# Reading the moving operand of every large product as pairs of columns 256 apart

## The chip, the cores and the metric

The kernel runs on one core of a Trainium2 chip. The metric is device time in microseconds (us) of one execution, the median of several. Every matmul goes to TensorE (PE in the profile), which keeps one operand in place (the weights, `lhsT`) and lets the other stream past it (the moving operand, `rhs`), one column after the other, into PSUM. VectorE (DVE), ScalarE (ACT) and GpSimd (POOL) do the rest, and SyncE (SP) issues all DMA transfers of this kernel.

## What is computed

A recurrent attention layer, followed by a two-layer network with SiLU between the layers. In the reference, cut to what matters:

```python
B, H, S, D = 4, 8, 768, 64
for t in range(S):
    state = gamma * state + einsum('bhd,bhe->bhde', k[:, :, t], v[:, :, t])
    y[:, :, t] = scale * einsum('bhd,bhde->bhe', q[:, :, t], state)
x = y.transpose(0, 2, 1, 3).reshape(B * S, H * D)      # 3072 x 512
h = x @ w_in                                           # 512 x 2048
out = (h * sigmoid(h)) @ w_out                         # 2048 x 512, out is 3072 x 512
```

## The kernel before

**Tokens.** The 768 steps are cut into 6 chunks c of 128 steps. One chunk of all 4 batch rows b makes 512 tokens, in the order b, then step: token number n of a chunk is step n mod 128 of batch row n div 128.

**Attention** (`stage_t`, `stage_s`, `stage_a`, `stage_y`, lines 471 to 606) works on units (c, b) with many small matmuls of 64 by 64 and leaves x transposed in `xt[c]`: 128 partitions, 4 slices `kk` of the 512 features, 512 tokens.

**Exact products out of a faster number type.** Every fp32 operand is split into a high part, a low part and a third part that combines them (`split_steps` for the weights, `split_x` for x, `split` for the middle values). Each product is made of three matmuls in fp32r: high and low go into one PSUM bank (`ha`, or `oa` at the end), the third into another (`hb`, `ob`), and the result is `ha * ONE_E - hb`.

**First product** (`multiply`, lines 743 to 751; `multiply_part`, lines 938 to 942, for the first few, which are woven into the attention by hand). For each chunk c and each of the 16 slices f of 128 middle features, 12 matmuls of 128x512: three parts by four `kk`. The weights are `w_sb[f]`, the moving operand is `xt[c][:, i, kk, :]`, 512 tokens. `close_steps` (lines 769 to 782) copies `ha` out on ACT, subtracts `hb` on DVE, applies SiLU on ACT, and SP writes the 128x512 result to DRAM (`gd`, line 791).

**Second product** (lines 1225 to 1249). For each chunk c and slice f, the middle values are read back (`gr`, line 804), split into three parts (`split`, lines 836 to 841), and each of the 4 blocks of 128 tokens (`ts(b, C)`) serves as weights of three matmuls of 128x512, whose moving operand is `wo[f][:, i, :]`, the 512 output columns. After 16 slices f, block b is complete in the banks `oa` and `ob`. ACT copies `oa` out (line 1288), DVE subtracts `ob` (line 1289), and SP stores 128 rows of 2 KB (line 1294). As the blocks are the batch rows, the 128 rows of a block are 128 consecutive rows of the output.

**The end** (lines 1251 to 1283). In the last chunk the last two slices f are multiplied block by block (line 1267), so that the first blocks are copied out while PE works on the others. The last block is done as a left and a right half of 256 columns, each finished by one DVE instruction (line 1281) and stored by its own DMA (line 1283).

**Order.** PE's order of instructions is written out by hand. In the first 56 us the other engines' order is, too; later their queues follow from calls like `tc.issue_after`. In the second half SP alternates between reading `gr`, which waits until a buffer has been split, and storing finished blocks.

Of the kernel before, what the change touches and what calls it, by code (L numbers as in the profile page):

```python
# [18 lines left out]
AF = mybir.ActivationFunctionType  # L19
ALU = mybir.AluOpType  # L20
# [10 lines left out]
ONE_E = 1.0 + EPS  # L31
# [3 lines left out]
def kernel(  # L35
# [28 lines left out]
    nc = tc.nc  # L64
    B, H, S, D = q.shape
    DM, DF = moe_w_in.shape
    C = 128
# [9 lines left out]
    scale = 1.0 / math.sqrt(D)  # L77
# [54 lines left out]
    def split_w(*of):  # L132
# [2 lines left out]
        yield  # L135
        list(steps)


    units = [(c, b) for c in range(NC) for b in range(B)]
    kqv = {"k": {}, "q": {}, "v": {}}  # L140
# [172 lines left out]
    def fill(out, n, start=True):  # L313

        cols = out.shape[-1] // 128
        for _ in range(n):
            nc.tensor.matmul(out, lhsT=zero, rhs=zero.unsqueeze(1).to_broadcast([128, cols, 128]),
                             start=start, stop=True, skip_group_check=True)
# [25 lines left out]
    for j in range(2):  # L344
        for a in range(HP):
            nc.scalar.activation(out=decay[:, j, a, :], in_=lag[:, :D], func=AF.Exp,
                                 scale=float(lg[2 * a + j]))
# [10 lines left out]
    for h in range(H):  # L358
        nc.scalar.activation(out=gk[:, 0, h : h + 1], in_=pos, func=AF.Exp,
                             scale=float(-lg[h]))  # L360
# [22 lines left out]
    xt, kt, qt, am = {}, {}, {}, {}  # L383
# [8 lines left out]
    def banks(tag, name, n=2):  # L392
        return ps_u.tile([128, n, 512], FP32, tag=tag, name=name)
# [3 lines left out]
    def turn(name):  # L397
        turns[0] += 1
        return ps_h.tile([128, 512], FP32, tag=f"h{turns[0] % 3}", name=name)
# [340 lines left out]
    def product_in(c, f):  # L740
        close_in(c, f, *multiply(c, f))

    def multiply(c, f):
        ha, hb = turn(f"ha_{c}_{f}"), turn(f"hb_{c}_{f}")
        fill(ha, FILL_P.get((c, f), 0))
        for i in range(3):
            for kk in range(KIN):
                nc.tensor.matmul(hb if i == 2 else ha, lhsT=w_sb[f][:, i, ts(kk, 128)],  # L748
                                 rhs=xt[c][:, i, kk, :], start=kk == 0 and i != 1,
                                 stop=kk == KIN - 1 and i != 0)  # L750
        return ha, hb

# [33 lines left out]
    def put_g(keep, of=None):  # L786
        of = pending if of is None else of
        while len(of) > keep:
            c, f, g = of.pop(0)
            with tc.issue_after(last[0]) if of is later else ExitStack():  # L790
                last[:] = stored[:] = [nc.sync.dma_start(out=g_dram[c, f], in_=g).ins]
# [3 lines left out]
    got, ready, wo, w_got = {}, {}, {}, {}  # L795
# [31 lines left out]
    def split(n):  # L827
        if n >= len(order):
            return
        c, f = order[n]  # L830
        get(n + G_AHEAD)
        g = got.pop(n)
        if f % 4 == 0:
            blocks[n // 4] = xpool.tile([128, 3, 4, NT], FP32R, tag="xt", name=f"gs_{c}_{f}")
        t = blocks[n // 4][:, :, f % 4, :]
        nc.scalar.activation(out=t[:, 0, :], in_=g, func=AF.Copy, scale=HALF)  # L836
        high = t[:, 0, :].bitcast(FP32)
        nc.vector.tensor_tensor(out=t[:, 1, :], in0=g, in1=high, op=ALU.subtract)  # L838
        nc.vector.scalar_tensor_tensor(out=t[:, 2, :], in0=t[:, 1, :].bitcast(FP32),  # L839
                                       scalar=-1.0 / EPS, in1=high,  # L840
                                       op0=ALU.mult, op1=ALU.add)
        ready[n] = t
# [95 lines left out]
    def multiply_part(c, f, into, steps):  # L938
        for i, kk in [(i, kk) for i in range(3) for kk in range(KIN)][steps]:
            nc.tensor.matmul(into[i == 2], lhsT=w_sb[f][:, i, ts(kk, 128)],  # L940
                             rhs=xt[c][:, i, kk, :], start=kk == 0 and i != 1,
                             stop=kk == KIN - 1 and i != 0)

    def PP(n, i):
# [277 lines left out]
                        split(f - NF + S_AHEAD)  # L1222
    put_g(0)

    for c in range(NC):
        acc = []
        for b in range(B):
            if b < 2:
                u = banks("sy"[b], f"o{b}_{c}")
                acc.append([u[:, i] for i in range(2)])  # L1230
            else:
                acc.append([turn(f"oa{b}_{c}"), turn(f"ob{b}_{c}") if b == 2 else
                            banks("q", f"ob{b}_{c}", 1)[:, 0]])
        early_f = NF if c < NC - 1 else NF - 2
        for f in range(NF):
            n = c * NF + f
            split(n + S_AHEAD)
            if n < 4:
                w_out(NF - 4 + n)
            t = ready[n]  # L1240
            if f >= early_f:
                continue
            for b in range(B):
                gh, glo, gm = (t[:, i, ts(b, C)] for i in range(3))
                oa, ob = acc[b]
                for o, g, i in (oa, gh, 0), (oa, glo, 1), (ob, gm, 2):
                    nc.tensor.matmul(o, lhsT=g, rhs=wo[f][:, i, :], start=f == 0 and i != 1,  # L1247
                                     stop=f == NF - 1 and i != 0 or
                                     (b, f, i) == (B - 1, early_f - 1, 1))

        ends = []
        if early_f < NF:
            left, right = (ts(i, DM // 2) for i in range(2))
            halves_of = [one.tile([128, DM // 2], FP32, tag="qt", name=f"o_{x}", bufs=3)
                         for x in ("left", "right")]
            nc.scalar.activation(out=halves_of[0], in_=acc[B - 1][0][:, left], func=AF.Copy,
                                 scale=ONE_E)
            last_left = banks("s", "oa_left")[:, 0]
            for b in (0, 1, B - 1, 2):
                ends.append((b, acc[b][1], (2,), slice(None)))  # L1260
                if b < B - 1:
                    ends.append((b, acc[b][0], (0, 1), slice(None)))
            ends += [(B - 1, last_left, (0, 1), left), (B - 1, acc[B - 1][0], (0, 1), right)]
        for b, o, parts, cols in ends:
            for f in range(early_f, NF):
                for i in parts:
                    nc.tensor.matmul(o[:, cols], lhsT=ready[c * NF + f][:, i, ts(b, C)],  # L1267
                                     rhs=wo[f][:, i, cols],
                                     start=o is last_left and (f, i) == (early_f, 0),
                                     stop=f == NF - 1 and i != 0,  # L1270
                                     skip_group_check=cols != slice(None))
        for b in range(B):
            oa, ob = acc[b]
            rows = ds(b * S + c * C, C)
            if c == NC - 1 and b == B - 1:
                nc.vector.tensor_tensor(out=halves_of[0], in0=halves_of[0], in1=ob[:, left],
                                        op=ALU.subtract)
                nc.scalar.copy(out=halves_of[1], in_=ob[:, right])
                for x, o, cols, op in ((last_left, halves_of[0], left, ALU.add),
                                       (oa, halves_of[1], right, ALU.subtract)):  # L1280
                    nc.vector.scalar_tensor_tensor(out=o, in0=x[:, cols], scalar=ONE_E, in1=o,
                                                   op0=ALU.mult, op1=op)
                    nc.sync.dma_start(out=out[rows, cols], in_=o)
                continue
            o = one.tile([128, DM], FP32, tag=("kt", "qt")[b % 2], name=f"o_{c}_{b}",
                         bufs=(2, 3)[b % 2])
            if c < NC - 1:
                nc.scalar.activation(out=o, in_=oa, func=AF.Copy, scale=ONE_E)  # L1288
                nc.vector.tensor_tensor(out=o, in0=o, in1=ob, op=ALU.subtract)
            else:  # L1290
                nc.scalar.copy(out=o, in_=ob)
                nc.vector.scalar_tensor_tensor(out=o, in0=oa, scalar=ONE_E, in1=o,
                                               op0=ALU.mult, op1=ALU.subtract)
            nc.sync.dma_start(out=out[rows, :], in_=o)


# [28 lines left out]
```

## Time and profile before

| | |
|---|---|
| time, median of 3 runs (lowest, highest) | 612.83 us (611.51, 613.1) |
| span of the profiled execution, first to last instruction | 609.7 us |
| difference of that median to the span, taken as what lies around the span | 3.1 us |
| PE busy with matmuls | 602.0 us, 99% of the span, 5509 instructions |
| DVE, ACT, POOL busy | 65%, 54%, 6% |
| DMA engines, mean share in 40 slices | 90% or more at the start, 30 to 50% in the second half |

The page of the profile does not give the profiled execution's own time; its span is the number that is compared. In lines of groups stand the kernel line, the engine, the operation, the tile written and the tiles read, the shape and the number of instructions, then the time in sum and the mean of one in nanoseconds. Matmuls are pipelined, so the duration of one (about 390 ns) is longer than the distance from one to the next; the distance has to be read from start times.

### The profile page before, as it was taken

To read this page: it belongs to the slowest core of one execution; us is meant where nothing else is said; L and a number is where in the kernel's file an instruction comes from. 1 tells how busy PE (TensorE), PEld (TensorE's weight loads), DVE (VectorE), ACT (ScalarE), POOL (GpSimd) and SP (SyncE) were. 2 spreads that over 40 slices of the span, in tenths; PEclk is the share of its full clock that TensorE was granted. 3 is DMA by queue.
4 is the path that set the end of the run, shared out by engine and by line. 5 is a ranking of instruction groups with operands and counts; after the bars stand their busy time and mean duration, and the time that the engine had idled before them with its cause. 6 is when DMAs were issued, how large, how long until landed. Compare 5 with 4: busy or idle time off the path is not lost.

```text
span 609.7 us, 13719 instructions
## 1 busy us (share of the span) xinstructions
PE 602.0 (99%) x5509; PEld 496.7 (81%) x5509; DVE 395.3 (65%) x672; ACT 326.4 (54%) x607; POOL 33.9 (6%) x89
## 2 busy tenths in 40 slices
PE   8999999999999999999999999999999999999997
PEld 6787888888888888888888888888888888888886
DVE  3888898678876766766699775635454553645632
ACT  7788777678766677666789622221221312313211
POOL 3000110100031111210000000000000000000000
PEclk9999999999999999999999999999999999999999
DMA  9997878876899699898777532524433432533301
GB/s 192 215 211 187 192 208 265 240 236 205 256 248 211 163 274 262 244 279 264 263 267 246 161 124 88 188 69 119 158 91 117 138 119 89 161 115 103 104 1 69
DMA packets 144334, 108.89 MB, mean 179 GB/s; under 512 B 101136, under 2 KB 109584, under 8 KB 144272
## 3 DMA queue, kind: packets, MB, share of 16 engines
q1 hardware_dynamic: 144272, 108.03, 62.6%
q8 instruction: 43, 0.70, 0.5%
q14 instruction: 19, 0.16, 0.1%
HBM read 66.06 MB, written 36.70 MB: 169 GB/s over the span
## 4 chain that ended last, share of the span: by engine, by line
PE 94%; SPq 2%; DMA 2%; ACT 1%; issue 0%; DVE 0%; POOL 0%; DVEq 0%; POOLq 0%
PE ha L748 28%; PE o L1247 21%; PE oa L1247 14%; PE hb L748 14%; PE ob L1247 7%; PE y L576 4%; SPq L166 2%; PE sc L518 2%; PE sc L528 2%; DMA kqv<-in_v_dram 1%; PE ha L940 1%; DMA wf<-in_moe_w_in_dram 1%; PE hb L940 0%; PE o L1267 0%; PE kp L486 0%; PE qp L486 0%
## 5 line engine op out<-in xcount | busy, mean ns | idle before, releaser
L748 PE MATMUL ha<-xt,wi 128*128 128x512 f32 x736 | 184.2, 392 | 0.0
L748 PEld LDWEIGHTS ha<-xt,wi 128*128 128x128 f32 x736 | 136.7, 188 | 29.0
L1247 PE MATMUL o<-wo,gs 128*128 128x512 f32 x564 | 143.1, 389 | 0.0
L836 ACT ACTIVATE gs<-gr 128x512 fp32r<-128x512 f32 x96 | 53.3, 621 | 139.0 <-issue 138.0
L1247 PEld LDWEIGHTS o<-wo,gs 128*128 128x128 f32 x564 | 105.8, 188 | 22.0
L838 DVE TENSOR_TENSOR gs<-gr,gs 128x512 fp32r<-128x512 f32 x96 | 62.1, 684 | 94.2 <-ACT gs L836 94.2
L1247 PE MATMUL oa<-wo,gs 128*128 128x512 f32 x376 | 115.7, 389 | 0.0
L748 PE MATMUL hb<-xt,wi 128*128 128x512 f32 x368 | 98.3, 389 | 0.0
L776 DVE TENSOR_TENSOR g<-g,hb 128x512 f32<-128x512 f32 x87 | 59.5, 684 | 52.7 <-ACT g L771 39.1
L1247 PEld LDWEIGHTS oa<-wo,gs 128*128 128x128 f32 x376 | 70.6, 188 | 14.7
L748 PEld LDWEIGHTS hb<-xt,wi 128*128 128x128 f32 x368 | 69.1, 188 | 14.4
L1247 PE MATMUL ob<-wo,gs 128*128 128x512 f32 x188 | 73.1, 389 | 0.0
L781 ACT ACTIVATE g<-g 128x512 f32<-128x512 f32 x87 | 54.9, 631 | 33.4 <-DVE g L776 33.2
L771 ACT ACTIVATE g<-ha 128x512 f32<-128x512 f32 x87 | 51.8, 596 | 26.7 <-PE ha L748 19.9
L839 DVE SCALAR_TENSOR_TENSOR gs<-gs 128x512 fp32r<-128x512 f32 x96 | 62.0, 683 | 0.1
L1247 PEld LDWEIGHTS ob<-wo,gs 128*128 128x128 f32 x188 | 35.3, 188 | 7.3
L205 ACT ACTIVATE ca<-wf 128x512 f32<-128x512 f32 x32 | 21.5, 673 | 7.3 <-DVE cs L218 2.9
L536 DVE TENSOR_TENSOR am<-sc,decay 128x512 f32<-128x512 f32 x24 | 16.5, 687 | 11.8 <-PE sc L528 10.5
L1288 ACT ACTIVATE o<-o 128x512 f32<-128x512 f32 x10 | 6.0, 600 | 33.4 <-PE o L1247 33.0
L218 DVE SCALAR_TENSOR_TENSOR cs<-ca,cs 128x512 uint32<-128x512 uint32 x32 | 23.1, 722 | 0.9
L576 PE MATMUL y<-qt,mid 64*64 64x64 f32 x376 | 19.5, 220 | 0.6 <-issue 0.5
L653 DVE SCALAR_TENSOR_TENSOR xt<-xt 128x512 fp32r<-128x512 f32 x28 | 19.7, 714 | 0.6
(137 smaller groups left out, 606.3 us busy)
## 6 DMA issues: line engine op xcount, KB each, us to landing
gr<-gd SPq DMA_DIRECT2D x96, 256.0 KB, 2.7
gd<-g SPq DMA_DIRECT2D x87, 256.0 KB, 3.6
wf<-in_moe_w_out_dram SPq DMA_DIRECT2D x16, 512.0 KB, 4.4
out_dram<-o SPq DMA_DIRECT2D x23, 256.0 KB, 2.1
wf<-in_moe_w_in_dram SPq DMA_DIRECT2D x16, 256.0 KB, 4.2
wf<-in_moe_w_in_dram SPq DMA_DIRECT2D x32, 128.0 KB, 3.9
kf<-in_k_dram SPq DMA_DIRECT2D x16, 256.0 KB, 4.1
qf<-in_q_dram SPq DMA_DIRECT2D x16, 256.0 KB, 4.1
```

Of the source, the lines that this page charges most:

```text
L205: top = nc.scalar.activation(out=a.bitcast(FP32), in_=hi.bitcast(FP32), func=AF.Abs, scale=2.0 ** -3).ins
L218: nc.vector.scalar_tensor_tensor(out=s, in0=a, scalar=3, in1=s, op0=ALU.logical_shift_left, op1=ALU.bitwise_xor)
L576: i = nc.tensor.matmul(to[ts(e, D), o, a, :], lhsT=lhsT, rhs=rhs, start=key not in started, stop=True, skip_group_check=True).ins
L653: nc.vector.scalar_tensor_tensor(out=x[2], in0=x[1].bitcast(FP32), scalar=-1.0 / EPS, in1=x[0].bitcast(FP32), op0=ALU.mult, op1=ALU.add)
L748: nc.tensor.matmul(hb if i == 2 else ha, lhsT=w_sb[f][:, i, ts(kk, 128)], rhs=xt[c][:, i, kk, :], start=kk == 0 and i != 1, stop=kk == KIN ...
L771: copied[:] = [nc.scalar.activation(out=hs, in_=ha, func=AF.Copy, scale=ONE_E).ins]
L776: taken_out[:] = [nc.vector.tensor_tensor(out=hs, in0=hs, in1=hb, op=ALU.subtract).ins]
L781: nc.scalar.activation(out=hs, in_=hs, func=AF.Silu)
L836: nc.scalar.activation(out=t[:, 0, :], in_=g, func=AF.Copy, scale=HALF)
L838: nc.vector.tensor_tensor(out=t[:, 1, :], in0=g, in1=high, op=ALU.subtract)
L839: nc.vector.scalar_tensor_tensor(out=t[:, 2, :], in0=t[:, 1, :].bitcast(FP32), scalar=-1.0 / EPS, in1=high, op0=ALU.mult, op1=ALU.add)
L1247: nc.tensor.matmul(o, lhsT=g, rhs=wo[f][:, i, :], start=f == 0 and i != 1, stop=f == NF - 1 and i != 0 or (b, f, i) == (B - 1, early_f - 1 ...
```

## The change

`woven` reads a row of 512 columns in the order 0, 256, 1, 257, 2, 258 and so on: pairs of columns that lie 256 apart, which in fp32r is 1,024 bytes. All large products take their moving operand that way. The number of matmuls, their shapes, their weights and their order on PE stay the same.

The consequences are carried along. In the first product the tokens of a chunk come out in woven order and stay so in `gd`: a block of 128 columns then holds 64 steps of two batch rows, alternating (rows b div 2 and 2 + b div 2, steps (b mod 2) * 64 onward). So a finished block of the second product is stored by two DMAs, one from the even and one from the odd partitions, 64 rows of 2 KB each (`store_out`). In the second product the output columns come out woven in PSUM; the instructions of ACT and DVE that copy them out read every second column (`unwoven`) and write two runs of 256 (`apart_cols`). The left half of the last block now holds columns 0 to 127 and 256 to 383, so its two DMAs store pieces of 512 bytes, and those of the right half too.

```diff
+    def woven(t):
+        return t.rearrange("p (o n) -> p n o", o=2)
...
                 nc.tensor.matmul(hb if i == 2 else ha, lhsT=w_sb[f][:, i, ts(kk, 128)],
-                                 rhs=xt[c][:, i, kk, :], start=kk == 0 and i != 1,
+                                 rhs=woven(xt[c][:, i, kk, :]), start=kk == 0 and i != 1,
...
+    def apart_cols(t):
+        return t.rearrange("p (o n) -> p o n", o=2)
+    def unwoven(t):
+        return t.rearrange("p (n o) -> p o n", o=2)
+    by_halves = out.rearrange("(o i s) d -> i s o d", o=2, i=B // 2)
+    def store_out(c, b, t, cols):
+        rows = ds(c * C + b % 2 * D, D)
+        for o in range(2):
+            nc.sync.dma_start(out=cols(by_halves[b // 2, rows, o]), in_=t[o::2])
...
                 for o, g, i in (oa, gh, 0), (oa, glo, 1), (ob, gm, 2):
-                    nc.tensor.matmul(o, lhsT=g, rhs=wo[f][:, i, :], start=f == 0 and i != 1,
+                    nc.tensor.matmul(o, lhsT=g, rhs=woven(wo[f][:, i, :]),
+                                     start=f == 0 and i != 1,
...
                     nc.tensor.matmul(o[:, cols], lhsT=ready[c * NF + f][:, i, ts(b, C)],
-                                     rhs=wo[f][:, i, cols],
+                                     rhs=woven(wo[f][:, i, :])[:, by_two[cols.start, cols.stop]],
...
+                    nc.vector.scalar_tensor_tensor(
+                        out=apart_cols(o[i]), in0=unwoven(x[:, cols]), scalar=ONE_E,
+                        in1=apart_cols(o[i]), op0=ALU.mult, op1=op)
+                    store_out(c, b, apart_cols(o[i]),
+                              lambda t: t.rearrange("s (o n) -> s o n", o=2)[:, :, ts(i, DM // 4)])
...
-                nc.scalar.activation(out=o, in_=oa, func=AF.Copy, scale=ONE_E)
-                nc.vector.tensor_tensor(out=o, in0=o, in1=ob, op=ALU.subtract)
+                nc.scalar.activation(out=oo, in_=unwoven(oa), func=AF.Copy, scale=ONE_E)
+                nc.vector.tensor_tensor(out=oo, in0=oo, in1=unwoven(ob), op=ALU.subtract)
...
-            nc.sync.dma_start(out=out[rows, :], in_=o)
+            store_out(c, b, o, lambda t: t)
```

More of the change, by code (lines that the diff above doesn't have):

```diff
@@ L940, in multiply_part @@
             nc.tensor.matmul(into[i == 2], lhsT=w_sb[f][:, i, ts(kk, 128)],
-                             rhs=xt[c][:, i, kk, :], start=kk == 0 and i != 1,
+                             rhs=woven(xt[c][:, i, kk, :]), start=kk == 0 and i != 1,
                              stop=kk == KIN - 1 and i != 0)
@@ L1252 @@
         if early_f < NF:
-            left, right = (ts(i, DM // 2) for i in range(2))
+            left, right = slice(0, DM // 2), slice(DM // 2, DM)
+            whole = slice(0, DM)
+            by_two = {(0, DM): slice(0, DM // 2), (0, DM // 2): ts(0, DM // 4),
+                      (DM // 2, DM): ts(1, DM // 4)}
             halves_of = [one.tile([128, DM // 2], FP32, tag="qt", name=f"o_{x}", bufs=3)
                          for x in ("left", "right")]
-            nc.scalar.activation(out=halves_of[0], in_=acc[B - 1][0][:, left], func=AF.Copy,
+            nc.scalar.activation(out=apart_cols(halves_of[0]),
+                                 in_=unwoven(acc[B - 1][0][:, left]), func=AF.Copy,
                                  scale=ONE_E)
@@ L1259 @@
             for b in (0, 1, B - 1, 2):
-                ends.append((b, acc[b][1], (2,), slice(None)))
+                ends.append((b, acc[b][1], (2,), whole))
                 if b < B - 1:
-                    ends.append((b, acc[b][0], (0, 1), slice(None)))
+                    ends.append((b, acc[b][0], (0, 1), whole))
             ends += [(B - 1, last_left, (0, 1), left), (B - 1, acc[B - 1][0], (0, 1), right)]
@@ L1267 @@
                     nc.tensor.matmul(o[:, cols], lhsT=ready[c * NF + f][:, i, ts(b, C)],
-                                     rhs=wo[f][:, i, cols],
+                                     rhs=woven(wo[f][:, i, :])[:, by_two[cols.start, cols.stop]],
                                      start=o is last_left and (f, i) == (early_f, 0),
                                      stop=f == NF - 1 and i != 0,
-                                     skip_group_check=cols != slice(None))
+                                     skip_group_check=cols != whole)
         for b in range(B):
             oa, ob = acc[b]
-            rows = ds(b * S + c * C, C)
             if c == NC - 1 and b == B - 1:
[L1276 to L1283, printed above, removed]
+                o = halves_of
+                nc.vector.tensor_tensor(out=apart_cols(o[0]), in0=apart_cols(o[0]),
+                                        in1=unwoven(ob[:, left]), op=ALU.subtract)
+                nc.scalar.copy(out=apart_cols(o[1]), in_=unwoven(ob[:, right]))
+                for i, (x, cols, op) in enumerate(((last_left, left, ALU.add),
+                                                   (oa, right, ALU.subtract))):
+                    nc.vector.scalar_tensor_tensor(
[3 more added lines that the diff above has]
+                              lambda t: t.rearrange("s (o n) -> s o n", o=2)[:, :, ts(i, DM // 4)])
                 continue
@@ L1286 @@
                          bufs=(2, 3)[b % 2])
+            oo = apart_cols(o)
             if c < NC - 1:
-                nc.scalar.activation(out=o, in_=oa, func=AF.Copy, scale=ONE_E)
-                nc.vector.tensor_tensor(out=o, in0=o, in1=ob, op=ALU.subtract)
-            else:
-                nc.scalar.copy(out=o, in_=ob)
-                nc.vector.scalar_tensor_tensor(out=o, in0=oa, scalar=ONE_E, in1=o,
+                nc.scalar.activation(out=oo, in_=unwoven(oa), func=AF.Copy, scale=ONE_E)
+                nc.vector.tensor_tensor(out=oo, in0=oo, in1=unwoven(ob), op=ALU.subtract)
+            else:
+                nc.scalar.copy(out=oo, in_=unwoven(ob))
+                nc.vector.scalar_tensor_tensor(out=oo, in0=unwoven(oa), scalar=ONE_E, in1=oo,
                                                op0=ALU.mult, op1=ALU.subtract)
-            nc.sync.dma_start(out=out[rows, :], in_=o)
+            store_out(c, b, o, lambda t: t)
 _INS = ['q', 'k', 'v', 'moe_w_in', 'moe_w_out']
```

## The prediction, made before the changed kernel ran

> **What bounds the kernel now.** I read the page first, for the engine that fills the span and for the chain that ended last, then the table by stretches of time, to see where PE has slack, and last the timeline, for the distance between matmuls.
>
> ```profile
> span 609.7 us, 13719 instructions
> PE 602.0 (99%) x5509; PEld 496.7 (81%) x5509; DVE 395.3 (65%) x672; ACT 326.4 (54%) x607; POOL 33.9 (6%) x89
> ...
> PEclk9999999999999999999999999999999999999999
> ...
> PE ha L748 28%; PE o L1247 21%; PE oa L1247 14%; PE hb L748 14%; PE ob L1247 7%; PE y L576 4%; SPq L166 2%; PE sc L518 2%; PE sc L528 2%; DMA kqv<-in_v_dram 1%; PE ha L940 1%; DMA wf<-in_moe_w_in_dram 1%; PE hb L940 0%; PE o L1267 0%; PE kp L486 0%; PE qp L486 0%
> ```
>
> PE is busy in 99% of the span, its clock is never held back, and the chain runs through the large matmuls: 28, 14, 21, 14 and 7% for lines 748 and 1247, 84% in sum. So whatever the change does to one such matmul counts nearly in full. The stretches say where it doesn't quite:
>
> ```profile
> 26.00:56.00 30.00, 28.64 (x673) 23.40 (x672) 24.49 (x45) 25.97 (x68) 0.36 (x4) 1.00 0.98 217
> 56.00:300.00 244.00, 244.00 (x2884) 201.82 (x2883) 184.13 (x317) 176.62 (x302) 28.29 (x40) 1.00 0.86 237
> 330.00:600.00 270.00, 270.00 (x1193) 223.58 (x1192) 142.43 (x232) 75.97 (x138) 0.00 (x0) 1.00 0.36 115
> ```
>
> After the times stand the busy time of PE, of its weight loads, of DVE, ACT and POOL, the granted clock and the share of the DMA engines. From 56 us on PE has no gap. Between 26 and 56 us the DMA engines are at 0.98, and PE waits now and then.
>
> How many matmuls the change touches is in the groups:
>
> ```profile
> L748 PE MATMUL ha<-xt,wi 128*128 128x512 f32 x736 | 184.2, 392 | 0.0
> L1247 PE MATMUL o<-wo,gs 128*128 128x512 f32 x564 | 143.1, 389 | 0.0
> L1247 PE MATMUL oa<-wo,gs 128*128 128x512 f32 x376 | 115.7, 389 | 0.0
> L748 PE MATMUL hb<-xt,wi 128*128 128x512 f32 x368 | 98.3, 389 | 0.0
> L1247 PE MATMUL ob<-wo,gs 128*128 128x512 f32 x188 | 73.1, 389 | 0.0
> L940 PE MATMUL ha<-xt,wi 128*128 128x512 f32 x32 | 9.0, 411 | 0.1
> L940 PE MATMUL hb<-xt,wi 128*128 128x512 f32 x16 | 4.3, 390 | 0.0
> ```
>
> ```profile
> L1267 PE MATMUL o<-wo,gs x12: 389/389/389, 600.3 to 602.8; 128*128 128x512 f32 x12
> L1267 PE MATMUL oa<-wo,gs x8: 279/336/389, 604.0 to 605.7; 128*128 128x512 f32 x4, 128*128 128x256 f32 x4
> L1267 PE MATMUL ob<-wo,gs x4: 389/389/389, 603.0 to 603.7; 128*128 128x512 f32 x4
> L1267 PE MATMUL oa_left<-wo,gs x4: 277/282/283, 604.9 to 605.2; 128*128 128x256 f32 x4
> ```
>
> That is 736 + 368 + 32 + 16 + 564 + 376 + 188 + 12 + 4 + 4 = 2300 matmuls of 512 columns and 8 of 256.
>
> **What one of them costs now.** The 389 ns is a matmul's latency. The distance is read from start times, of a run of twelve and of four narrow ones:
>
> ```profile
> 592.17 1.52 PE L1247 MATMUL o<-wo,gs 128*128 128x512 f32 x6
> ...
> 594.89 0.39 PE L1247 MATMUL o<-wo,gs 128*128 128x512 f32 x1
> ```
>
> ```profile
> 604.86 0.64 PE L1267 MATMUL oa_left<-wo,gs 128*128 128x256 f32 x4
> 605.33 0.64 PE L1267 MATMUL oa<-wo,gs 128*128 128x256 f32 x4
> ```
>
> Between 592.17 and 594.89 lie 6 of `o`, then two, one, two and one of `oa` and `ob`: 12 in 2.72 us, 226.7 ns each. The four of 256 columns take 0.47 us, 117.5 ns each. The difference, 109.2 ns for 256 columns, is 0.427 ns a column, and 226.7 - 512 x 0.427 leaves 8 ns that doesn't depend on the width. So the moving operand streams at 0.43 ns a column. 2300 x 226.7 ns is 521 us, 86% of the span, which fits the chain.
>
> **The change, part by part. First the reads of the moving operand,** the only term that matters. No instruction of this trace lets two neighbouring reads fall 1,024 bytes apart, so its price has to be bounded. What other readers take per element is here:
>
> ```profile
> L1291 ACT COPY o<-o x2: 587/587/587, 601.9 to 603.2; 128x512 f32<-128x512 f32 x2
> ```
>
> ```profile
> L1278 ACT COPY o_right<-ob x1: 375/375/375, 604.6 to 604.6; 128x256 f32<-128x256 f32 x1
> ```
>
> ```profile
> 50.67 0.60 PE L486 MATMUL qp<-ident,qf 128*128 128x128 f32 x4
> 51.10 0.59 PE L317 MATMUL ha<-zero 128*128 128x512 bf16 x2
> ```
>
> ACT's second 256 elements cost 587 - 375 = 212 ns, 0.83 ns each. PE's transposes, each with 128 columns of fresh fp32 weights, follow one another every 0.43 us / 4 = 107.5 ns; 128 streamed columns would be 128 x 0.427 = 55 ns, so it is the weights that set this pace, at 0.84 ns a column. The moving operand alone is twice as fast as either. My reading is that it gets there because one fetch brings neighbouring columns, and that pairs 256 apart take this away: then each column costs a fetch of its own, at the 0.83 to 0.84 ns of the other readers.
>
> Lower end, a gain: the most that a better read order could take away is what lies above the streaming. The dummy matmuls in bf16, which read 128 columns four times over, show such a case:
>
> ```profile
> L317 PE MATMUL sc<-zero 128*128 128x512 bf16 x3 | 0.8, 379 | 0.0
> ```
>
> ```profile
> 12.15 0.81 PE L317 MATMUL sc<-zero 128*128 128x512 bf16 x3
> ```
>
> Two distances fit into 0.81 - 0.379 us: 215.5 ns each, 11.2 ns under the 226.7 of the large products. So the fixed part may be 11.2 rather than 8 ns, and the cost of the read order lies between -11.2 ns and, with 512 x 0.84 + 11.2 = 441.3 ns, +214.6 ns for a matmul. I take 512 x 0.84 + 8 = 438.1 ns, +211.4 ns: of the two rows of plain readers it is that of PE itself. For 256 columns it is 256 x 0.84 + 8 - 117.5 = +105.5 ns.
>
> One rule bears on this. The Trainium skill, page "Advanced Engine Details and Errata", section "Memory Cachelines", says that SBUF has lines of 16 bytes and that a reader needs at least two hits on a line to absorb the latency of the memory, with a penalty when every access is to another line; woven, each access is to another line, so by that rule the matmuls get slower, but it gives no size. What this trace has of strided reads stops short of the case:
>
> ```profile
> L208 DVE TENSOR_SCALAR cs<-wf x32: 411/420/428, 9.8 to 327.1; 128x512 uint32<-128x512 uint32 x32
> ```
>
> ```profile
> L214 DVE TENSOR_SCALAR ca<-ca x32: 411/420/427, 10.5 to 327.4; 128x512 f32<-128x512 f32 x32
> ```
>
> ```profile
> L205 ACT ACTIVATE ca<-wf x32: 653/672/703, 9.8 to 321.4; 128x512 f32<-128x512 f32 x32
> ```
>
> ```profile
> L836 ACT ACTIVATE gs<-gr x96: 614/618/640, 302.0 to 585.8; 128x512 fp32r<-128x512 f32 x96
> ```
>
> Lines 208 and 205 read every second word of their tile, 8 bytes apart; lines 214 and 836 read without gaps. On DVE the stride is free (420 ns both times); on ACT it goes with 672 against 618 ns, 54 ns for 512 elements, if the whole difference is due to it. Strides of 8 bytes are thus no disaster, and leave the question of 1,024 bytes open.
>
> **Copying out and storing.** ACT and DVE now read PSUM at every second column when they copy blocks out. By the rows above that is 0 to 54 ns for an instruction, 40 instructions in chunks 0 to 4, under PE's unbroken run from 330 to 600 us: nothing, as long as banks come free in time. Without that cover it would be 40 x 54 ns = 2.2 us. The extra DMA of each block is one more issue on SP. What it waits behind and what waits behind it:
>
> ```profile
> SPq L804 <- DVE gs L838: 154.3, 87, 7.5
> ```
>
> SP spends 154 us waiting for buffers of the reads `gr`, so one issue of a third of a microsecond per block, 20 of them before the last chunk, delays only reads that are four slices ahead: nothing.
>
> At the very end there is no cover:
>
> ```profile
> 603.22 2.94 SPq L1294 DMA_DIRECT2D out_dram<-o  x3
> 606.26 0.39 SPq L1283 DMA_DIRECT2D out_dram<-o_left  x1
> 606.74 0.40 SPq L1283 DMA_DIRECT2D out_dram<-o_right  x1
> ```
>
> ```profile
> L1294 SPq DMA_DIRECT2D out_dram<-o x23: 332/337/338, 387.7 to 605.8; - x23
> ```
>
> The last whole block was issued until 603.22 + 2.94 = 606.16, and needs 0.34 us more for its second half: 606.50. Then four issues of 0.39 to 0.40 us instead of two: until 606.50 + 1.58 = 608.08, against 606.74 + 0.40 = 607.14 now. That is +0.9 us, from where the last transfer lands as before (609.7 - 607.1 = 2.6 us after its issue). Pieces of 512 bytes instead of 1 KB may add a little; I take none.
>
> **The head.** The 48 matmuls of line 940 grow by 48 x 211.4 ns = 10.1 us in the stretch from 26 to 56 us, in which PE stands idle for 30 - 28.6 = 1.4 us and DMA is at 0.98. Between none and all of it may be hidden by transfers that are late anyway; I take 3 us off.
>
> **The sum.** 2300 x 211.4 ns = 486.2 us, 8 x 105.5 ns = 0.8 us, the end 0.9 us, the head -3 us: +484.9 us. 609.7 + 484.9 = 1094.6 us of span, and with the 3.1 us around it (612.8 - 609.7) 1097.7 us. With the larger fixed part and nothing hidden it is 2300 x 214.6 ns + 1.7 us = 495.3 us more: 1108 us, 1110 with the spread of the runs. At ACT's 0.83 ns, with the fixed 8 ns gone behind the slower stream and the head hiding all 10 us, it is 2300 x 198.3 ns + 1.7 - 10 = 447.8 us more: 1061 us. So this case by itself reaches from 1061 to 1110.
>
> **Rivals.** *Faster: the read order removes the fixed part.* The distance falls from 226.7 towards the 215.5 ns of the dummies: 2300 x 11.2 ns = 25.8 us less, plus 0.9 at the end, 587.9 us. For it: those dummies read a two-level pattern (128 columns, four times) and are the only 512-column matmuls at this pace. Against: they also have bf16 weights, and nothing says which of the two does it. It decides as soon as a pair costs no second fetch, since then only the fixed part is left to change. *No change: the reader doesn't care.* Two lines held at once would serve both columns of a pair and their neighbours. Then only the end is left: 612.8 + 0.9 = 613.7 us, +0.15%. *Slower, but mildly:* a stride costs what it may cost ACT, 54 ns for 512 elements: 2300 x 54 ns + 0.9 us = 125 us, 738 us. For it: the only row in which a stride seems to cost anything. Against: it is another engine with half the pace, which has time to spare. *Worse than one fetch a column,* if a fetch that misses isn't even pipelined: above 1110 us; no row shows a reader slower than 0.84 ns on PE or ACT. That the pattern isn't carried out as written I leave out: the tokens of a chunk would come out in another order than they are stored.
>
> **From cases to numbers.** One fetch a column 0.47, mild 0.13, above 1110 us 0.04: slower by over 0.3% 0.64. No change 0.08. Faster 0.28, at about 588 us. Runs here differ by 1.6 us, so 0.3% is about what a measurement can tell. The predicted time is that of the likeliest case, 1097.7 us. Without the faster case more than 2 in 10 would be left out, so the range goes from 586, 2 us under that case's time for the spread of the runs, to 1110; the likeliest case's own range is 1061 to 1110.
>
> **What the changed profile would show.** Right: distances near 438 ns between starts of lines 748 and 1247, the same 2300 and 8 matmuls, PE still without gaps after 56 us, more idle time on ACT and DVE, a lower DMA share, the clock still full. The last two stores as four issues of 0.4 us. Wrong: distances of 227 ns or less (the fetch isn't what sets the pace), distances in between (a fetch still serves some neighbours), or a span that doesn't grow with the distances because something outside PE hid them.

## The result, and the profile after

The changed kernel takes 604.52 us (603.2 to 605.5) against 612.75 us (611.51 to 613.1) before: a ratio of 0.9868, 95% interval 0.985 to 0.9886. I had forecast 1097.7 us. The profiled execution's span fell from 609.7 to 601.2 us.

From the page of the kernel after: the span, the busy time of the engines, the granted clock, and the groups of the large matmuls (mean of one in nanoseconds before the second bar, idle time before them behind it).

```profile
span 601.2 us, 13742 instructions
PE 583.6 (97%) x5509; PEld 496.5 (83%) x5509; DVE 400.8 (67%) x672; ACT 333.1 (55%) x607; POOL 34.3 (6%) x89
...
PEclk9999999999999999999999999999999999999999
...
L752 PE MATMUL ha<-xt,wi 128*128 128x512 f32 x736 | 177.7, 384 | 1.1 <-DVE g L780 0.9
L1267 PE MATMUL o<-wo,gs 128*128 128x512 f32 x564 | 137.1, 379 | 0.0
...
L752 PE MATMUL hb<-xt,wi 128*128 128x512 f32 x368 | 96.1, 384 | 5.6 <-ACT g L775 3.7
```

The matmuls are the same in number, and each has become shorter: 379 ns where 389 stood. The distance from start to start is in the timeline of PE after:

```profile
579.83 0.81 PE L1267 MATMUL o<-wo,gs 128*128 128x512 f32 x3
580.48 0.59 PE L1267 MATMUL oa<-wo,gs 128*128 128x512 f32 x2
580.91 0.38 PE L1267 MATMUL ob<-wo,gs 128*128 128x512 f32 x1
581.13 0.59 PE L1267 MATMUL oa<-wo,gs 128*128 128x512 f32 x2
581.56 0.38 PE L1267 MATMUL ob<-wo,gs 128*128 128x512 f32 x1
581.77 1.46 PE L1267 MATMUL o<-wo,gs 128*128 128x512 f32 x6
```

From 579.83 to 581.77 are 9 matmuls, 215.6 ns each: 11.1 ns less than the 226.7 before. 2300 times that would be 25.5 us, but the span lost only 8.5. The first and last starts of the two products, before and after, show where the rest stayed. First the kernel before, then the one after, each by its source lines (three durations, then first and last start):

```profile
L748 PE MATMUL ha<-xt,wi x736: 389/389/501, 55.8 to 343.5; 128*128 128x512 f32 x184
L748 PE MATMUL hb<-xt,wi x368: 388/389/392, 57.6 to 344.4; 128*128 128x512 f32 x184
...
L1247 PE MATMUL ob<-wo,gs x188: 389/389/389, 346.5 to 600.1; 128*128 128x512 f32 x188
```

```profile
L752 PE MATMUL ha<-xt,wi x736: 379/379/484, 56.3 to 345.0; 128*128 128x512 f32 x184
L752 PE MATMUL hb<-xt,wi x368: 379/379/483, 58.0 to 345.9; 128*128 128x512 f32 x184
...
L1267 PE MATMUL ob<-wo,gs x188: 379/379/379, 347.8 to 589.3; 128*128 128x512 f32 x188
```

The second product went from 253.6 to 241.5 us, the whole of its 1128 x 11 ns. The first product gained nothing: 288.6 us from first to last start before, 289.6 after, though its 1104 matmuls are 12 us cheaper. PE waits there now. Before, the table of waits named no wait of line 748; after, the waits of PE's weight loads (PEld) include these (us in total, times, longest):

```profile
PEld hb L752 <- ACT g L775: 8.6, 15, 2.1
PEld ha L752 <- DVE g L780: 6.2, 17, 0.9
```

PE waits until ACT and DVE have emptied a PSUM bank. And some instructions on ACT and DVE have become slower that the change doesn't touch: those that read every second word of the weights as they were loaded (lines 205, 208 and 212 before, 209, 212 and 216 after). Two of them after the change (shortest, median and longest duration, first and last start):

```profile
L209 ACT ACTIVATE ca<-wf x32: 682/872/1010, 9.9 to 324.5; 128x512 f32<-128x512 f32 x32
L212 DVE TENSOR_SCALAR cs<-wf x32: 420/519/1335, 9.9 to 330.2; 128x512 uint32<-128x512 uint32 x32
```

The medians were 672 and 420 ns; they are 872 and 519. ACT's readers without gaps did not slow down: the SiLU of line 785 (781 before), in the same stretch, took 632 ns on average against 631, and line 840 (836 before) 620 against 621. At the end, SP's timeline after:

```profile
596.30 1.22 SPq L1243 DMA_DIRECT2D out_dram<-o_left  x2
597.61 1.21 SPq L1243 DMA_DIRECT2D out_dram<-o_right  x2
```

The last issue ends at 598.82 us, 4.2 us after the last matmul's start at 594.6; before, it was 607.14 - 605.7 = 1.4 us. In sum, from start to start: head +0.5, first product +1.0, from there to the first `ob` of the second -0.2, second product -12.1, its last two slices -0.3, the end +2.5 (6.5 us from the start of the last matmul to the end of the span, against 4.0): -8.5 us, to 0.1.

### The profile page after: what moved, and what is told of

It reads as the page before. It is cut to its first block, busy times and chain, and to the rows that moved or that the text cites. A ratio compares the mean times of both kernels' runs of the same rounds, so it can differ in the third digit from the quotient of the medians.

```text
span 601.2 us, 13742 instructions
## 1 busy us (share of the span) xinstructions
PE 583.6 (97%) x5509; PEld 496.5 (83%) x5509; DVE 400.8 (67%) x672; ACT 333.1 (55%) x607; POOL 34.3 (6%) x89
## 5 line engine op out<-in xcount | busy, mean ns | idle before, releaser
L752 PE MATMUL ha<-xt,wi 128*128 128x512 f32 x736 | 177.7, 384 | 1.1 <-DVE g L780 0.9
L1267 PE MATMUL o<-wo,gs 128*128 128x512 f32 x564 | 137.1, 379 | 0.0
L1267 PE MATMUL oa<-wo,gs 128*128 128x512 f32 x376 | 111.8, 379 | 0.0
L752 PE MATMUL hb<-xt,wi 128*128 128x512 f32 x368 | 96.1, 384 | 5.6 <-ACT g L775 3.7
L1267 PE MATMUL ob<-wo,gs 128*128 128x512 f32 x188 | 71.3, 379 | 0.0
L209 ACT ACTIVATE ca<-wf 128x512 f32<-128x512 f32 x32 | 26.6, 830 | 12.1 <-DVE cs L222 7.6
L657 DVE SCALAR_TENSOR_TENSOR xt<-xt 128x512 fp32r<-128x512 f32 x28 | 21.9, 795 | 0.6
```

What stands on the lines that cost most here:

```text
L209: top = nc.scalar.activation(out=a.bitcast(FP32), in_=hi.bitcast(FP32), func=AF.Abs, scale=2.0 ** -3).ins
L657: nc.vector.scalar_tensor_tensor(out=x[2], in0=x[1].bitcast(FP32), scalar=-1.0 / EPS, in1=x[0].bitcast(FP32), op0=ALU.mult, op1=ALU.add)
L1267: nc.tensor.matmul(o, lhsT=g, rhs=woven(wo[f][:, i, :]), start=f == 0 and i != 1, stop=f == NF - 1 and i != 0 or (b, f, i) == (B - 1, earl ...
```

## The experiments

Three questions: what makes a matmul 11 ns cheaper, why the first product doesn't profit, and what the end costs. All kernels were made from the one before the change, except w2_pair, which was made from the changed one.

**Each product alone.** w2_pair keeps the change in the second product and takes it back in the first, with its stores in one DMA. w1_pair does it the other way round.

```diff
 w2_pair, against the changed kernel
-                                 rhs=woven(xt[c][:, i, kk, :]), start=kk == 0 and i != 1,
+                                 rhs=xt[c][:, i, kk, :], start=kk == 0 and i != 1,
...
-        for o in range(2):
-            nc.sync.dma_start(out=cols(by_halves[b // 2, rows, o]), in_=t[o::2])
+        nc.sync.dma_start(out=cols(out[rows]), in_=t)
```

> Only the second product reads its moving operand in pairs 256 apart; the first reads as before, so tokens keep their order and each block is stored by one DMA. Theory A (each woven matmul is 10.9 ns cheaper everywhere, and the first product's stage hands its share back because ACT and DVE don't keep up there): the second product keeps its 12.5 us, so about 600.5 us, and the instructions that read every second word of the weights stay at 420 ns on DVE and 672 on ACT. Rival (the gain in the second product hangs on what the first one does, the chunks merely starting earlier): less than 5 us gained, above 607 us.

Measured: 600.85 us (599.94 to 601.57) against 612.41, ratio 0.9803, interval 0.9781 to 0.9824. The readers stayed at 421 and 672 ns; the last of them starts at 331 us, before the second product begins. Theory A holds, and half of the change is better than the whole.

> Only the first product reads in pairs; the second as before, rows stored in two DMAs. Theory A: matmul distances of lines 748 fall to 216 ns, but the stage from 56 to 345 us keeps its length within 2 us, because PE waits for ACT and DVE instead; with the longer end about 613 to 616 us. The readers of every second word go to about 520 ns on DVE and 870 on ACT, as with both products woven. Rival (the slow-down of those readers comes from somewhere else, such as the order of DMAs): they stay at 420 and 672 ns and the time falls towards 603 us.

Measured: 617.27 us, ratio 1.0101, interval 1.0048 to 1.0154, slower than the kernel before and a little worse than expected. The matmuls of the first product are at 216 ns. Its source lines, and then the group of the reader on ACT:

```profile
L751 PE MATMUL ha<-xt,wi x736: 379/379/483, 56.6 to 345.8; 128*128 128x512 f32 x184
L751 PE MATMUL hb<-xt,wi x368: 379/379/484, 58.4 to 346.7; 128*128 128x512 f32 x184
```

```profile
L208 ACT ACTIVATE ca<-wf 128x512 f32<-128x512 f32 x32 | 26.6, 832 | 10.8 <-DVE cs L221 6.7 <-DMA wf<-in_moe_w_out_dram 3.4 <-DMA wf<-in_moe_w_in_dram 0.7
```

It is 290.1 us from start to start, and the reader on ACT takes 832 ns on average against 673 before. So the first product alone, read in pairs, slows them.

**Does that slow-down hold PE up?** w1_gapless and its control gapless read neighbouring words instead. They take the low and the high words from the two halves of the tile and lower a bound of the exponent, so their weights are other numbers:

```diff
-        words = t.rearrange("p (c w) -> p c w", w=2)
-        lo, hi = words[:, :, 0], words[:, :, 1]
+        lo, hi = t[:, :DM], t[:, DM:]
```

> First product in pairs, as in w1_pair, but the conversion of the weights reads 512 neighbouring words instead of every second one (low and high words are the two halves of the tile, the bound of the exponent is lowered to keep numbers finite; the weights are then other numbers). Theory S (the slowed readers of every second word on ACT and DVE hold PE up in the first product): the readers stay near 420 and 640 ns, PE's waits there vanish, and the stage from 56 to 345 us gets 10 to 13 us shorter; about 604 us. Theory C (ACT and DVE can't take results out faster in any case): the readers are fast again and the stage still lasts 288 to 290 us, so about 615 us.

> Control: the kernel before, with the same conversion that reads 512 neighbouring words and the same other numbers. Matmuls stay at 227 ns and PE has no gap to close, so both theories expect no change beyond 1 us from 612.5 us; what differs from that has to be taken off from w1_gapless.

Measured: 606.11 us and, for the control, 612.33 us (one run each). The first product of w1_gapless, then of gapless, and last the reader on ACT in w1_gapless:

```profile
L750 PE MATMUL ha<-xt,wi x736: 379/379/484, 56.0 to 335.6; 128*128 128x512 f32 x184
L750 PE MATMUL hb<-xt,wi x368: 379/379/483, 57.8 to 336.5; 128*128 128x512 f32 x184
```

```profile
L747 PE MATMUL ha<-xt,wi x736: 387/389/501, 56.3 to 344.1; 128*128 128x512 f32 x184
L747 PE MATMUL hb<-xt,wi x368: 388/389/395, 58.2 to 345.0; 128*128 128x512 f32 x184
```

```profile
L207 ACT ACTIVATE ca<-wf x32: 612/630/641, 10.1 to 315.5; 128x512 f32<-128x512 uint32 x32
```

280.5 against 288.7 us: with these readers the first product keeps 8.2 of its 12 us, and takes 9.6 us less than in w1_pair (290.1). Read without gaps they take 630 ns on ACT, 629 in the control, so the pairs don't slow them. In the waits of w1_gapless between 56 and 345 us, those for ACT and DVE (lines 773 and 778) fell to 2.4 and 1.9 us, from 9.0 and 6.3 in w1_pair. So theory S holds in direction: how long these readers take bears on what PE can keep. But 630 ns is also less than the 672 of the kernel before, so the 9.6 us are more than the slow-down alone costs; w1_near below separates the two.

**What makes a matmul cheaper.** Six other orders for the moving operand, in the second product only. Each run replaces the pattern in one helper:

```diff
+    def arranged(t):
+        return t.rearrange("p (o n r) -> p n o r", o=2, r=128)   # w2_block
+        return t.rearrange("p (o n) -> p n o", n=4)              # w2_stride: n is outer, o inner
+        return t.rearrange("p (o n r) -> p n o r", o=2, r=2)     # w2_two
+        return t.rearrange("p (m o n) -> p m n o", o=2, n=4)     # w2_near
+        return t.rearrange("p (m o n) -> p m n o", o=2, n=2)     # w2_cross
+        return t.rearrange("p (n o) -> p o n", o=2)              # w2_even
...
-                    nc.tensor.matmul(o, lhsT=g, rhs=wo[f][:, i, :], start=f == 0 and i != 1,
+                    nc.tensor.matmul(o, lhsT=g, rhs=arranged(wo[f][:, i, :]), start=f == 0 and i != 1,
```

The pattern of w2_stride takes, for each of four n, all 128 columns that lie four apart: 0, 4, 8 and so on. Its expectation describes it otherwise, as four places 128 columns apart in turn; what ran are single reads 16 bytes from one to the next. The six were run once each.

> Second product only: four runs of 128 neighbouring columns in the order 0, 2, 1, 3, so there are two levels in the pattern but neighbours in one line; the output's columns are left in the order in which they were multiplied. Theory of levels (any pattern of more than one level is served without the fixed 11 ns): distance 216 ns, about 600 us. Theory of lines (neighbouring reads have to fall into different lines): 227 ns, about 612.7 us.

> Second product only: columns 128 apart, four of them in turn, so again no two neighbouring reads in one line, but with four places instead of two; the output's columns are left in that order. Theory of lines: 216 ns as with pairs, about 600 us. Rival (a reader holds two lines, so two places are served and four are not): the distance grows, towards 440 ns if each column costs a fetch, then above 800 us.

> Second product only: runs of two neighbouring columns, taken in turn from two places 256 columns apart; the output's columns are left in that order. If it is the alternation between two places from column to column that counts, the fixed part comes back at least in part (between 216 and 227 ns); if it is enough that two lines are read in turn within a short time, 216 ns, about 600 us.

> Second product only: pairs of columns 4 apart (16 bytes), within groups of 8 neighbouring columns; the output's columns are left in that order. If two places of any distance are served at once, 216 ns and about 600 us; if the two have to lie far apart (in different parts of the memory), 227 ns or more, 612 us or above.

> Second product only: order 0, 2, 1, 3 within each group of four columns, so a pair is not neighbouring but lies in one line of 16 bytes; the output's columns are left in that order. Theory P (columns at even and at odd places of the order come through a line buffer each; the fixed 11 ns are lost where both want the same line): 227 ns, about 612 us. Rival (it is enough that the two columns of a pair are not neighbours): 216 ns, about 600 us.

> Second product only: all even columns, then all odd ones, 8 bytes from one to the next; the output's columns are left in that order. Theory P: at each place, even or odd, every read is in another line, so it is slow as with quads (460 ns) or as with runs of two (340 ns), time 740 to 880 us. Rival (two hits on a line in a row are enough, whatever the place): 216 to 227 ns, 600 to 613 us.

The group of `o` in the second product, in the order w2_near, w2_block, w2_cross, w2_two, w2_even, w2_stride, one view of each:

```profile
L1252 PE MATMUL o<-wo,gs 128*128 128x512 f32 x564 | 137.1, 379 | 0.0
```

```profile
L1252 PE MATMUL o<-wo,gs 128*128 128x512 f32 x564 | 143.1, 389 | 0.0
```

```profile
L1252 PE MATMUL o<-wo,gs 128*128 128x512 f32 x564 | 143.1, 389 | 0.0
```

```profile
L1252 PE MATMUL o<-wo,gs 128*128 128x512 f32 x564 | 208.0, 513 | 0.0
```

```profile
L1252 PE MATMUL o<-wo,gs 128*128 128x512 f32 x564 | 272.8, 632 | 0.0
```

```profile
L1252 PE MATMUL o<-wo,gs 128*128 128x512 f32 x564 | 276.2, 639 | 0.0
```

| order of the columns | distance, ns | time, us |
|---|---|---|
| 0, 1, 2, 3 (before) | 227 | 612.8 |
| 0, 256, 1, 257 (w2_pair) | 216 | 600.9 |
| 0, 4, 1, 5 (w2_near) | 216 | 600.0 |
| four runs of 128 (w2_block) | 227 | 614.1 |
| 0, 2, 1, 3 (w2_cross) | 227 | 612.4 |
| 0, 1, 256, 257, 2, 3 (w2_two) | 340 | 743.8 |
| 0, 2, 4, 6 (w2_even) | 451 to 459 | 872.6 |
| 0, 4, 8, 12 (w2_stride) | 460 | 881.2 |

Levels in the pattern do nothing by themselves (w2_block), nor does it matter how far apart a pair lies (w2_near). My first idea, that neighbouring reads only have to fall into different places, fell with w2_two, for which I had expected 227 ns at most, and with w2_stride. A second one, theory P, fits all the rows of this table: take the columns at even places of the order and those at odd places as two streams. Where each stream moves on through its columns one by one, each in its own line of 16 bytes, it is 216 ns; where both streams walk through the same line, 227; where a stream changes its line with every read, 340 to 460. It was formed after w2_two and foretold w2_cross and the direction of w2_even. That there are two buffers behind it is an inference, and it doesn't say why w2_two is so much faster than w2_even. Nor does it cover the bf16 dummies of the prediction, which read neighbours in sequence and still take 215.5 ns.

**Which pairs disturb the readers.** The same orders in the first product, where tokens are shuffled within a block and the rows stored in two DMAs:

```diff
+    def shuffled(t):
+        return t.rearrange("p (m o n) -> p m n o", o=2, n=4)     # w1_near; n=2 in w1_cross
...
-                                 rhs=xt[c][:, i, kk, :], start=kk == 0 and i != 1,
+                                 rhs=shuffled(xt[c][:, i, kk, :]), start=kk == 0 and i != 1,
...
-            nc.sync.dma_start(out=out[rows, :], in_=o)
+        for o in range(2):
+            nc.sync.dma_start(out=rows.rearrange("(m o n) d -> o m n d", o=2, n=4)[o], in_=t[o::2])
```

> First product only, pairs of tokens 4 apart (16 bytes) within groups of 8; rows stored by two DMAs. Distance 216 ns by theory P. If the slowed readers of ACT and DVE come from the 1,024 bytes within a pair (one bank of the memory), they stay at 672 and 420 ns and the first stage gets about 10 us shorter: about 605 us. If they come from pairs as such, they go to about 870 and 520 ns as in w1_pair, and the time is about 616 us.

> First product only, order 0, 2, 1, 3 within four tokens, rows stored by two DMAs. By theory P nothing changes on PE (227 ns) and the readers of every second word stay at 672 and 420 ns; with the longer end about 615 us. By the rival 216 ns; the readers then tell whether a pair in one line disturbs them.

Measured: 609.69 and 614.61 us (one run each, 612.63 beside them for the kernel before). From w1_near, the same two views:

```profile
L751 PE MATMUL ha<-xt,wi x736: 379/379/483, 56.1 to 339.0; 128*128 128x512 f32 x184
L751 PE MATMUL hb<-xt,wi x368: 379/379/483, 57.9 to 339.9; 128*128 128x512 f32 x184
```

```profile
L208 ACT ACTIVATE ca<-wf 128x512 f32<-128x512 f32 x32 | 21.5, 672 | 11.1 <-DVE cs L221 6.6 <-DMA wf<-in_moe_w_out_dram 3.4 <-DMA wf<-in_moe_w_in_dram 1.1
```

Pairs 16 bytes apart are just as cheap on PE, leave the reader on ACT at 672 ns, and the first product takes 283.8 us instead of 290.1. These 6.3 us go with the slowed readers. But it is only 4.9 us less than before, where I had expected ten: the other 7 of the 12 us are lost although no reader is slowed. PE still waits for ACT and DVE there (5.6 and 2.8 us), and ACT in turn waits for a transfer to DRAM that has yet to free a buffer:

```profile
ACT g L774 <- DMA gd<-g: 11.1, 12, 2.0
```

In the kernel before, this wait is 1.8 us; it is 8.8 in w1_gapless. Whether it is what holds up the rest was not tested. w1_cross stayed at 227 ns and 289.0 us, and its readers at 672 and 420 ns.

**Both products, without the disturbance.** The last three run both products in pairs: tokens 64 apart (both_64) or 4 apart (both_near, both_near_act) in the first, columns 256 apart in the second, 128 apart in the last block so that its halves stay whole.

```diff
+    def paired(t, n):
+        return t.rearrange("p (h o n) -> p h n o", o=2, n=n)
...
-                                 rhs=xt[c][:, i, kk, :], start=kk == 0 and i != 1,
+                                 rhs=paired(xt[c][:, i, kk, :], 4), start=kk == 0 and i != 1,   # 64 in both_64
...
-                    nc.tensor.matmul(o, lhsT=g, rhs=wo[f][:, i, :], start=f == 0 and i != 1,
+                    nc.tensor.matmul(o, lhsT=g, rhs=columns(wo[f][:, i, :], c, b), start=f == 0 and i != 1,
```

> Both products in pairs: tokens 64 apart within a batch row (256 bytes) in the first, columns 256 apart in the second (128 apart in the last block, so that its halves stay whole); one DMA stores a block. If only pairs 1,024 bytes apart disturb the readers of every second word: they stay near 672 and 420 ns, and with 5 to 6 us from the first product and 12.5 from the second it is 593 to 596 us. If 256 bytes disturb them as well: 870 and 520 ns, and 600 to 602 us. If the end is longer only because of two DMAs, it is at most 1 us longer than in the kernel before (4.0 us from the start of the last matmul).

> As both_64, but tokens 4 apart (16 bytes) in the first product, and two DMAs of every second partition to a block, all on SP. Readers of every second word at 672 and 420 ns as in w1_near; first stage about 5 us shorter than before, second 12.5 us, the end 2 us longer: 596 to 598 us.

> As both_near, with the second DMA of each block of the last chunk on ACT's queue. If the longer end comes from issues one behind the other on SP, it loses 1 to 2 us of it: 594.5 to 597 us. If it comes from the transfers themselves, it is as both_near.

Measured: both_64 603.04 us, ratio 0.9832 (0.9805 to 0.9859); both_near 597.8 us, 0.9748 (0.9716 to 0.9779); both_near_act 598.85 us, 0.9748 (0.9699 to 0.9797). The reader on ACT, in both_64 and then in both_near:

```profile
L217 ACT ACTIVATE ca<-wf 128x512 f32<-128x512 f32 x32 | 26.6, 832 | 12.5 <-DVE cs L230 7.3 <-DMA wf<-in_moe_w_out_dram 2.9 <-DMA wf<-in_moe_w_in_dram 2.1
```

```profile
L217 ACT ACTIVATE ca<-wf 128x512 f32<-128x512 f32 x32 | 21.5, 673 | 11.6 <-DVE cs L230 6.2 <-DMA wf<-in_moe_w_out_dram 3.2 <-DMA wf<-in_moe_w_in_dram 2.2
```

Pairs 256 bytes apart disturb as much as those 1,024 apart, and both_64 loses 3.5 us in the first product (292.1 against 288.6 before) where w1_near gains 4.9; it came out above both of its expected ranges. both_near and both_near_act have the lowest times of all, lower than the change and than w2_pair. As for the end, SP's timeline of both_64, with one DMA for a store:

```profile
598.14 0.55 SPq L1239 DMA_DIRECT2D out_dram<-o_left  x1
598.79 0.57 SPq L1239 DMA_DIRECT2D out_dram<-o_right  x1
```

Its end, from the start of the last matmul, is 4.6 us, against 4.0 before and 6.5 after the change. It is 6.3 us in w1_pair (two DMAs, pieces of 1 KB) and 4.6 in w2_pair (one DMA, pieces of 512 bytes). So the second DMAs cost about 2 of the 2.5 us. both_near_act is inconclusive as a time: in its profile the end is 5.4 us against 6.6 in both_near, but its first product took 4.0 us longer, and its median missed the expected range. The granted clock accounts for a part of that. The stretch from 250 to 300 us in both_near_act, then in both_near (after the busy times the clock, the DMA share and GB/s):

```profile
250.00:300.00 50.00, 47.90 (x577) 40.68 (x576) 31.69 (x57) 33.76 (x56) 4.32 (x7) 0.97 1.01 281
```

```profile
250.00:300.00 50.00, 48.56 (x587) 41.45 (x586) 32.43 (x59) 34.05 (x56) 4.32 (x7) 1.00 1.02 287
```

Near 264 us, eight matmuls in a row of both_near_act are 426 to 452 ns apart instead of 216, 1.7 us in all. One of its four executions took 593.42 us, the others 598.58 to 599.96; what ACT's queue is worth stays open.

## Why the prediction was wrong

**The step that failed** is the second half of the reading that the moving operand is fast because one fetch brings neighbouring columns, and that "pairs 256 apart take this away". The term of the sum was +211.4 ns for a matmul, 486.2 us in all; it measured -11.1 ns. Pairs don't take it away: two places are served at full pace at every distance tried in pairs (16, 256 and 1,024 bytes). That skipping neighbours can cost this much fits the runs: w2_stride shows 460 ns and w2_even 451 to 459 where I had 438, but for other orders. I had bounded the price from both sides and then chosen the row by likeness of engine, where no row bore on the question. That 604.5 us lies between 586 and 1110 is no merit: the range spans two cases 500 us apart, and none of the cases put a time between 588 and 613.

**Smaller terms.** The 117.5 ns for 256 columns came from the first four, whose first step is short (113 ns); in the trace the later ones are 119.5 to 120 ns apart. With 119.7 the part that doesn't depend on the width is about 13 ns instead of 8, which would have moved the sum by some 5 ns a matmul. And what lies around the span is about 2.0 us, not 3.1: the profiled execution after the change took 603.2 us with a span of 601.2.

**The rule on lines.** The Trainium skill, "Advanced Engine Details and Errata", section "Memory Cachelines", asks for at least two hits on a line. The measurements differ on both sides: woven columns never hit the same line twice in succession and run faster than before, and w2_even, with two hits on each line in a row, takes twice as long. The measurement decides.

**The rival "faster"** had the mechanism on PE: 215.5 ns foretold, 215.6 measured. But its 587.9 us missed by 17 us, mostly since I let the whole gain through in the first product. The stretch table had DVE at 184 and ACT at 177 of 244 us there; this rival's sum took that for slack enough and didn't ask what a faster PE would wait for next, nor that an engine not touched by the change could become slower. Of the two things I thought might make the dummies fast, a pattern of two levels is not enough in fp32r (w2_block, 227 ns), and bf16 is not needed (w2_near, 216 ns). Why the dummies reach this pace in sequence stays open. Nor is what the pairs remove quite a fixed part: the eight matmuls of 256 columns took 832 ns from first to last start before and 779 after, 8 ns less each, against 11 ns for 512 columns.

**The end** was mis-sized: +0.9 us foretold, +2.5 measured. The number of issues was right, their price not; the source lines of the stores before and after:

```profile
L1294 SPq DMA_DIRECT2D out_dram<-o x23: 332/337/338, 387.7 to 605.8; - x23
```

```profile
L1243 SPq DMA_DIRECT2D out_dram<-o x46: 472/582/588, 387.1 to 595.6; - x46
```

An issue that stores every second partition takes SP 582 ns, not 337. both_64 has 0.55 us as well, with all partitions in one DMA whose rows alternate in DRAM. So it goes with the shape of the transfer; which part of the shape costs was not tested. The pieces of 512 bytes, which I took at nothing, go with 0.6 us in w2_pair (4.6 against 4.0 us).

**What held:** 2300 and 8 matmuls, distances of 226.7 ns, the clock at full speed, and that copying out and the extra stores cost nothing under PE's run in the second product, where line 1267 shows no idle time. The head, where I took off 3 us of a loss, moved by half a microsecond.

## What to carry to other kernels

A price that no row bears on is a coin to be tossed, not a term to be chosen by likeness; where one short run would tell, the forecast hangs on it. When the bounding engine gets faster in two stages, ask for each stage what it waits for next: here one stage kept everything and the other nothing, and taking the change back in that other one was better than the whole. When an experiment removes a disturbance, check that it doesn't also make something faster than it was before. And look for instructions elsewhere that become slower by what an engine now reads, by comparing durations group by group.

## What the runs showed of the hardware

Reading fp32r columns in single alternation from two places (0, 256, 1, 257 or 0, 4, 1, 5) takes 216 ns for 512 columns instead of 227 in sequence; every other order tried was no faster, and some took twice as long. PE's reads and those of ACT and DVE are not independent: with pairs 256 or 1,024 bytes apart, instructions that read every second word slowed from 673 to 832 ns on ACT on average, while the same instructions without gaps kept their pace (630 ns with pairs, 629 without). Pairs 16 bytes apart did no such harm (672 ns). The Trainium skill, "SBUF — State Buffer", section "Who interferes with whom", says that PE and ACT never wait on anyone; these runs differ, by 159 ns an instruction on ACT. Why the distance within a pair matters to ACT and not to PE, no run shows.
